# Loading the q and k weights into both partition halves, pairs of x blocks, and a new order, in an attention plus gMLP kernel

## The chip, the cores and the metric

The kernel runs on one core of one Trainium2 chip. The metric is the device time of one execution in microseconds (us), lower is better. Each run has a profiled span (first to last instruction), in most runs some 1.8 us shorter than its time, and the mean clock that TensorE was granted (1.0 is full speed). A run more than 1.5% above the fastest of the same kernel is called slow and left out of the ratios. "PE" is TensorE. The kernel before takes 255.0 us, the median of three runs (254.49 to 255.3).

## The reference, cut to what matters

```python
def reference(A_x, A_wqkv, A_wo, B_x, B_w_in, B_w_sp, B_b_sp, B_w_out):
    # S = 2048 tokens, D = 448, 16 heads of 28; bf16
    x = A_x
    h  = x + A(layernorm(x))     # q, k, v = x @ wqkv; each token attends to 8 keys,
                                 # itself and every second one before it; then @ wo
    h2 = h + B(layernorm(h))     # z = gelu(h @ w_in); g = w_sp @ layernorm(z[..., 896:]) + b_sp
    return h2                    # (z[..., :896] * g) @ w_out
```

The second part (gMLP with the 2048 x 2048 spatial weights) is dense matmul work and some 60% of the time. The change touches the start and the attention.

## The kernel before: the parts that matter

The program puts the two halves of the sequence (1024 tokens each) side by side: partitions 0 to 63 of the transposed, normalised x (`xh`) hold 64 features of the first half, partitions 64 to 127 the same features of the second. So each projection is two matmuls with 64 rows, and the weights must lie in both partition halves. Before, they were loaded once, with rows 0 to 383 across 128 partitions, and the PE copied each piece to both halves with a selector matrix (`dup`); ScalarE then moved it out of PSUM and padded each head from 28 to 32 columns.

```python
def ld_x(b, prio, eng="sp"):                       # one 128-token block of x
    t_x[b] = dma(eng, "x%d" % b, lambda e: e.dma_start(x_tm[:, b, :], X[128 * b:128 * b + 128, :]), ...)
# ... cut ...
t_w["qk", 0] = dma("act", "wqk0", lambda e: e.dma_start(
    stqk[:, 0:3, :], A_wqkv[0:384, 0:2 * D].rearrange("(c p) n -> p c n", p=128)), ...)
t_w["qk", 1] = dma("sp", "wqk1", lambda e: e.dma_start(stqk[0:64, 3, :], A_wqkv[384:448, 0:2 * D]), ...)
# ... cut ...
for h in hs:                                       # copies one piece to both halves
    iss("pe", lambda e, h=h: e.matmul(psum[:, bk[h] * 512:bk[h] * 512 + D], dup[64 * h:64 * h + 64, :],
                                      stqk[64 * h:64 * h + 64, j, c0:c0 + D]), ...)
# ... cut: ScalarE (one piece: VectorE) copies PSUM to wqp or wkp, 28 of every 32 columns ...
NWARM = 11                                         # idle matmuls at the very start
# ... cut ...
pace = [by[n % i] for i in range(4, NT) for n in ("exp%d_0", "mask%d", "ot%d")]
chain([t_wsp[b][0] for b in S_ORDER], pace, depth=2)   # spatial weights' transposing loads
```

x is normalised block by block on VectorE (`bn1`, `nrm1`). Blocks 0 to 2 of each half are transposed by the PE (`tT1`), blocks 3 to 7 by transposing DMA loads on SyncE's queue (`tD1`). One fixed list per engine gives the order of everything (`dp..` are the weight copies on the PE, `rp..` their padding, `mmq`, `mmk` and `mmv` the projections, `mml` logits, `ev..` evictions from PSUM):

```python
ORDER = {
    "sp":  """xhalo x0 x3 x11 x10 x1 x2 wqk1 x9 ... tD1_3 x4 x5 tD1_6 tD1_7 tD1_5 tD1_4 wsp0_0 ...""",
    "dve": """... bn1_14 mask0 bn1_15 bn1_5 bn1_4 nrm1_6 nrm1_14 nrm1_7 nrm1_5 nrm1_15 nrm1_13 evk1_1 nrm1_4 nrm1_12 ...""",
    "act": """x8 wqk0 rsh rs1_0 wv1 rpk1 rpk0 rpk2 ev1_0 rpk3 rpq0 rpq1 rpq2 evk0_0 ...""",
    "pe":  """warm dpk1 dpk0 tTh dpq0 dpk2 tT1_0 ... mmk0_0 dpq2 mmk0_2 mmq0_0 mmq0_2 tT1_2 tT1_1 mml0_00 mml0_01 mmv0 ...""",
}   # cut
```

The softmax here doesn't subtract the row's maximum and nothing guards it: scores larger than these inputs give would overflow.

## Time and profile before

| | kernel before |
|---|---|
| time, median of 3 | 255.0 us |
| profiled span, granted clock | 254.4 us, 1.000 |
| q and k weights landed | 6.75 us (the large part) |
| first q or k projection | 11.07 us |
| dense part, PE full | from 97.76 us to the end |

A profile line of a stretch gives its start and end, its length, then the busy time (and count) of PE, PE weight loads, VectorE, ScalarE and GpSimd, then the granted clock, the mean share of the 16 DMA engines that were busy, and GB/s. The chain is the work that ended last, followed backwards: each line is a start, a length, and what it was. The text below shows these views of the kernel before. One more of them is needed later, the same stretches microsecond by microsecond while the q and k weights fly (6 to 7) and after them (8 to 9):

```profile
6.00:7.00 1.00, 0.20 (x2) 0.11 (x4) 0.74 (x2) 0.00 (x0) 0.00 (x0) 1.00 1.09 371
...
8.00:9.00 1.00, 0.80 (x9) 0.49 (x9) 0.93 (x4) 1.00 (x3) 0.44 (x2) 1.00 1.07 258
```

The DMA engines are as busy in one as in the other; what differs is how much a busy engine moves.

### The profile page before, as it was taken

What the parts mean: (1) busy time and instruction counts of PE and PEld (TensorE: products, weight loads), DVE (VectorE), ACT (ScalarE), POOL (GpSimd) and SP (SyncE); (2) the same over time, 40 slices, a digit from 0 to 9 for tenths busy, and PEclk for the clock granted to TensorE, in tenths of its full rate; (3) what the DMA queues carried; (4) which work ended last, traced back from release to release, by engine and by line L of the source; (5) the groups of instructions that cost most, each with busy time, mean ns of one, the idle gap of its engine ahead of it and who ended that gap; (6) DMA issues with size and microseconds to landing.
All of it is one profiled execution on the core that took longest, in us unless ns stands there. A gap on an engine that the chain in (4) does not pass through costs nothing.

```text
span 254.4 us, 6475 instructions
## 1 busy us (share of the span) xinstructions
PE 240.2 (94%) x2906; PEld 120.0 (47%) x2917; DVE 144.4 (57%) x281; ACT 89.4 (35%) x105; POOL 27.7 (11%) x72
## 2 busy tenths in 40 slices
PE   7699979899997999999999999999999999999995
PEld 2375544455754544444444444444444444444452
DVE  7997755668796869998694013064700214424743
ACT  3878445555866785875644000000000000000000
POOL 5404300001020102201531000000000000000000
PEclk9999999999999999999999999999999999999999
DMA  6980892135688784399999900006000000010122
GB/s 218 260 107 4 156 153 67 21 78 143 118 116 84 125 129 73 72 130 194 231 186 170 201 3 0 3 0 124 0 3 18 0 0 0 25 50 0 54 66 82
DMA packets 55412, 22.03 MB, mean 87 GB/s; under 512 B 46664, under 2 KB 55256, under 8 KB 55384
## 3 DMA queue, kind: packets, MB, share of 16 engines
q1 hardware_dynamic: 51952, 16.79, 37.0%
q10 hardware_dynamic: 3432, 4.82, 9.0%
q8 instruction: 23, 0.38, 0.7%
q14 instruction: 5, 0.04, 0.1%
HBM read 8.39 MB, written 1.84 MB: 40 GB/s over the span
## 4 chain that ended last, share of the span: by engine, by line
PE 86%; DMA 5%; ACT 4%; DVE 3%; issue 1%; ACTq 0%
PE psum L1105 38%; PE psum L807 9%; PE psum L1134 8%; PE psum L1068 8%; PE psum L1005 8%; PE psum L985 4%; PE psum L847 3%; PE psum L882 3%; DMA xh<-tring 3%; DMA z2p<-in_A_wqkv_dram 2%; ACT reg L650 2%; PE psum L931 2%; ACT reg L895 1%; DVE reg L902 1%; PE psum L911 1%; DVE reg L949 1%
## 5 line engine op out<-in xcount | busy, mean ns | idle before, releaser
L1115 DVE TENSOR_TENSOR ub<-psum,reg 128x512 bf16<-128x512 f32 x28 | 18.7, 688 | 59.3 <-PE psum L1105 59.0
L1105 PE MATMUL psum<-reg,z2p 128*128 128x512 bf16 x218 | 48.8, 379 | 0.3
L1105 PE MATMUL psum<-wspT_lo,z2p 128*128 128x512 bf16 x219 | 48.1, 379 | 0.4 <-issue 0.2
L1105 PEld LDWEIGHTS psum<-wspT_lo,z2p 128*128 128x128 bf16 x224 | 21.8, 98 | 26.6 <-DVE z2p L1052 0.4
L1105 PEld LDWEIGHTS psum<-reg,z2p 128*128 128x128 bf16 x224 | 21.9, 98 | 26.1
L807 PE MATMUL psum<-xh,reg 64*128 64x128 bf16 (+3 forms) x336 | 26.9, 306 | 2.9 <-DMA xh<-tring 1.9
L650 ACT ACTIVATE reg<-psum 128x896 bf16<-128x896 f32 (+5 forms) x26 | 20.7, 851 | 7.2 <-PE psum L807 5.2
L1005 PE MATMUL psum<-w_in,xh 64*128 64x448 bf16 x224 | 22.7, 349 | 0.4 <-DVE reg L949 0.4
L895 ACT ACTIVATE reg<-psum 128x928 bf16<-128x928 f32 x18 | 17.0, 944 | 15.9 <-PE psum L847 7.1
L1134 PE MATMUL psum<-reg 128*128 128x448 bf16 x112 | 22.3, 352 | 0.1
L1068 PE MATMUL psum<-xh,w_in 64*128 64x512 bf16 x196 | 21.8, 376 | 0.0
L1142 DVE TENSOR_TENSOR tring<-psum,x_tm 128x448 bf16<-128x448 f32 x16 | 9.9, 622 | 17.9 <-PE psum L1134 17.8
L1036 DVE BATCH_NORM_STATS2 st<-z2p 128x6 f32<-128x448 bf16 x32 | 17.7, 609 | 3.9 <-ACT z2p L1030 3.9
L669 DVE BATCH_NORM_STATS2 st<-x_tm 128x6 f32<-128x448 bf16 x32 | 19.4, 606 | 0.4 <-DMA x_tm<-in_A_x_dram 0.3
L807 PEld LDWEIGHTS psum<-xh,reg 64*128 64x128 bf16 x336 | 13.2, 94 | 12.4 <-DMA xh<-tring 2.0
L656 POOL TENSOR_TENSOR rs<-rs,nhalf 128x2 f32<-128x2 f32 x23 | 16.6, 722 | 2.0
L1078 ACT ACTIVATE reg<-psum 128x1024 bf16<-128x1024 f32 x14 | 13.9, 1024 | 7.4 <-PE psum L1068 7.4
L652 DVE CAST reg<-psum 128x1024 bf16<-128x1024 f32 (+3 forms) x11 | 12.0, 1095 | 7.8 <-PE psum L807 6.2
L655 POOL TENSOR_SCALAR rs<-mv 128x2 f32<-128x2 f32 x23 | 5.2, 227 | 102.6 <-DVE mv L670 83.7
L1134 PEld LDWEIGHTS psum<-reg 128*128 128x128 bf16 x112 | 11.0, 98 | 10.6
L902 DVE TENSOR_TENSOR reg<-reg,mband 128x1856 bf16<-128x1856 bf16 x9 | 10.1, 1124 | 9.6 <-ACT reg L895 9.6
L1005 PEld LDWEIGHTS psum<-w_in,xh 64*128 64x128 bf16 x224 | 10.6, 94 | 10.3 <-issue 0.6
(68 smaller groups left out, 212.6 us busy)
## 6 DMA issues: line engine op xcount, KB each, us to landing
w_in<-in_B_w_in_dram ACTq DMA_DIRECT2D x4, 448.0 KB, 6.0
out_dram<-tring SPq DMA_DIRECT2D x16, 112.0 KB, 1.7
x_tm<-in_A_x_dram SPq DMA_DIRECT2D x15, 112.0 KB, 5.0
w_in<-in_B_w_in_dram ACTq DMA_DIRECT2D x4, 336.0 KB, 4.1
reg<-in_B_w_out_dram SPq DMA_DIRECT2D x1, 784.0 KB, 5.9
z2p<-in_A_wqkv_dram ACTq DMA_DIRECT2D x1, 672.0 KB, 5.5
reg<-in_B_b_sp_dram SPq DMA_DIRECT2D x1, 512.0 KB, 5.7
reg<-in_A_wqkv_dram ACTq DMA_DIRECT2D x1, 392.0 KB, 7.3
```

What stands on the lines that cost most here:

```text
L650: iss("act", lambda e: e.activation(dst, src, AF.Copy), reads=rd, writes=wr, after=after)
L656: iss("pool", lambda e: e.tensor_tensor(dst, dst, nh, ALU.pow), reads=rr + [r_nhalf], writes=rr)
L669: iss("dve", lambda e: e.bn_stats(st[:, b, :], x_tm[:, b, :]), reads=[r_x[b]], writes=[rl[b]])
L807: iss("pe", lambda e, c=c, s=s, gi=gi, lhs=lhs: e.matmul(psum[:, bk[s] * 512 + cw * gi:bk[s] * 512 + cw * gi + cw], lhs, xh[64 * s:64 * s ...
L895: iss("act", lambda e: e.activation(E[:, es[0], 2 * n:2 * n + 2, :], pair_view(lb, 0, 8 * JW), AF.Exp, scale=SCALE), reads=[r_bank[lb[0]], ...
L1005: iss("pe", lambda e, c=c, s=s: e.matmul(psum[:, zb[s] * 512:zb[s] * 512 + D], xh[64 * s:64 * s + 64, c, XO + 128 * u:XO + 128 * u + 128], ...
L1036: iss("dve", lambda e, b=b: e.bn_stats(st3[:, b, k, :], z2p[:, b, D * k:D * k + D]), reads=[r_z2[b][k]], writes=[r_st3[b][k]])
L1068: iss("pe", lambda e, c=c, s=s: e.matmul(psum[:, bk[s] * 512:bk[s] * 512 + 512], w_in[64 * s:64 * s + 64, c, 128 * f:128 * f + 128], xh[64 ...
L1078: iss("act", lambda e: e.activation(z1p[f].rearrange("p (s t) -> p s t", s=2)[:, :, 512 * ch:512 * ch + 512], pair_view(bk, 0, 512), AF.Ge ...
L1105: iss("pe", lambda e, b=b: e.matmul(psum[:, gb[0] * 512:gb[0] * 512 + 512], z2p[:, b, 128 * f:128 * f + 128], src[:, b, 512 * (tc % 2):512 ...
L1115: iss("dve", lambda e: e.tensor_tensor(ub[:, us_[0], :], psum[:, gb[0] * 512:gb[0] * 512 + 512], bb[:, 512 * tc:512 * tc + 512], ALU.add), ...
L1134: iss("pe", lambda e, f=f: e.matmul(psum[:, wb[0] * 512:wb[0] * 512 + D], z1p[f][:, 128 * m:128 * m + 128], w_out[:, f, :], start=(f == 0) ...
```

## The change

The intent: take the copying of weights off the PE and out of PSUM, by loading them twice, straight to both halves, and padding from SBUF on whichever of three engines is free; load x in larger pieces; hold the spatial weights' transposes back to tile 6 of the attention; and use the new order that the program's own planner makes of this. The diff, cut to its core:

```diff
-        def ld_x(b, prio, eng="sp"):
-            t_x[b] = dma(eng, "x%d" % b, lambda e: e.dma_start(x_tm[:, b, :], X[128 * b:128 * b + 128, :]), ...)
+        def ld_x(u, prio, eng="sp"):
+            t_x[u] = t_x[u + 8] = dma(eng, "x%d" % u, lambda e: e.dma_start(
+                x_tm[:, u:u + 9:8, :], X.rearrange("(s b p) d -> p b s d", s=2, p=128)[:, u]), ...)
 # ... cut ...
-        t_w["qk", 0] = dma("act", "wqk0", ...)      # rows 0 to 383, 128 partitions
-        t_w["qk", 1] = dma("sp", "wqk1", ...)       # rows 384 to 447
+        for j, (c0, c1) in enumerate(((0, 4), (4, NC7))):
+            for sd, eng in ((0, "sp"), (1, "act")):
+                t_w["qk", sd, j] = dma(eng, "wqk%d%d" % (sd, j), lambda e, sd=sd, c0=c0, c1=c1: e.dma_start(
+                    stqk[64 * sd:64 * sd + 64, c0:c1, :], A_wqkv[64 * c0:64 * c1, 0:2 * D].rearrange("(c p) n -> p c n", p=64)), ...)
 # ... cut: dup and its 14 matmuls removed ...
+                    copy(tk[0].eng, (wkp if p == "k" else wqp)[:, c0:c1, :].rearrange("p c (h d) -> p c h d", d=32)[:, :, :, 0:DH],
+                         stqk[:, c0:c1, o:o + D].rearrange("p c (h d) -> p c h d", d=DH), ...)   # on VectorE, ScalarE or GpSimd
 # ... cut ...
-        pace = [by[n % i] for i in range(4, NT) for n in ("exp%d_0", "mask%d", "ot%d")]
+        pace = [by[n % i] for i in range(6, NT) for n in ("exp%d_0", "mask%d", "ot%d")]
 # ... the order lists, cut to their heads ...
-    sp: xhalo x0 x3 x11 x10 x1 x2 wqk1 x9 ... tD1_3 x4 x5 tD1_6 tD1_7 tD1_5 tD1_4
+    sp: xhalo x1 x0 x3 wqk01 wqk00 x2 x7 wv0 x4 x5 x6 tD1_3 tD1_6 tD1_5 tD1_4 tD1_7
-    act: x8 wqk0 rsh rs1_0 wv1 rpk1 rpk0 rpk2 ev1_0 rpk3 rpq0 rpq1 rpq2 evk0_0
+    act: tab wqk11 rsh wqk10 wv1 rs1_0 rpk3 rpq2 rpq1 ev1_0 rpk0 rpk1 ev1_1 evq0_0
-    dve: ... bn1_14 mask0 bn1_15 bn1_5 bn1_4 nrm1_6 nrm1_14 ... nrm1_13 evk1_1 nrm1_4 nrm1_12
+    dve: ... bn1_12 nrm1_6 nrm1_14 mask0 nrm1_5 bn1_4 nrm1_13 nrm1_7 nrm1_4 nrm1_15 nrm1_12
-    pe: warm dpk1 dpk0 tTh ... mmk0_0 dpq2 mmk0_2 mmq0_0 mmq0_2 tT1_2 tT1_1 mml0_00
+    pe: warm tTh tT1_0 tT1_1 mmq0_0 mmq0_2 mmk0_2 mmk0_0 tT1_2 mmv0 mml0_00
```

## The prediction

> **What bounds the kernel now.** I read the page first, for the busy shares and the slices.
>
> ```profile
> PE 240.2 (94%) x2906; PEld 120.0 (47%) x2917; DVE 144.4 (57%) x281; ACT 89.4 (35%) x105; POOL 27.7 (11%) x72
> PE   7699979899997999999999999999999999999995
> PEclk9999999999999999999999999999999999999999
> GB/s 218 260 107 4 156 153 67 21 78 143 118 116 84 125 129 73 72 130 194 231 186 170 201 3 0 3 0 124 0 3 18 0 0 0 25 50 0 54 66 82
> ```
>
> TensorE is busy for 94% of 254.4 us at the full clock. Its low digits lie in the first two slices (up to 12.7 us), in the sixth and near 80 us. Only holes of this kind can be closed by moving loads and repacking. So I cut the span into four stretches (view of busy time by stretch: us, then PE, PEld, DVE, ACT, POOL, clock, DMA share, GB/s; the first of these rows is from another answer).
>
> ```profile
> 0.00:11.07 11.07, 7.30 (x37) 2.65 (x39) 9.12 (x27) 6.12 (x11) 5.42 (x28) 1.00 0.87 233
> ...
> 29.80:37.20 7.40, 5.54 (x176) 3.45 (x168) 5.35 (x5) 3.46 (x4) 0.00 (x0) 1.00 1.16 170
> 37.20:97.76 60.56, 56.32 (x1380) 30.66 (x1382) 43.57 (x61) 40.27 (x44) 4.56 (x10) 1.00 0.61 101
> 97.76:133.70 35.94, 35.82 (x350) 16.96 (x352) 30.98 (x76) 22.30 (x26) 10.06 (x22) 1.00 0.82 146
> 133.70:251.60 117.90, 117.30 (x549) 54.59 (x558) 39.76 (x77) 2.80 (x3) 0.70 (x1) 1.00 0.20 41
> ```
>
> From 97.76 us (the last output projection of attention, then gMLP) the PE is full to the end: 153.8 us that no load shortens. The attention stretch has 60.56 - 56.32 = 4.2 us idle, and 29.8 to 37.2 has 1.9. Then the chain that ended last, for the start:
>
> ```profile
> 1.25 5.50 DMA z2p<-in_A_wqkv_dram
> ...
> 6.80 0.41 PE psum L764 x2
> 7.23 2.54 ACT reg L650 x3
> 9.77 0.81 ACT xh L650
> 10.58 2.07 ACT reg L650 x3
> ...
> 12.69 2.52 PE psum L807 x84
> ...
> 29.80 7.36 DMA xh<-tring
> ```
>
> The start is a chain: the q/k weights land at 6.75, the PE copies them to both halves (L764), ScalarE pads seven of the eight pieces out of PSUM, and projections (L807) begin at 11.07, in earnest at 12.69. Later the chain runs through the transposing loads of normalised x. Last, the PE's waits within 11 to 98 us:
>
> ```profile
> PE psum L911 <- DVE reg L902: 2.2, 3, 1.1
> PE psum L807 <- DMA xh<-tring: 1.9, 1, 1.9
> PE psum L807 <- ACT reg L650: 1.1, 2, 0.6
> ```
>
> One DMA wait of 1.9 us, 1.1 us of waits for ScalarE copies (repacking among them), and 2.2 us of waits for the masked exponentials, which the change doesn't address.
>
> **What the Trainium skill says.** "DMA: Bandwidth & Descriptors", section "Rules for kernel authors", advises against two transfers to disjoint partition halves, since both spread over the same 16 DMA engines and serialize. So the second copy of the weights is paid in full, in bytes; the trace agrees in so far as the early DMA share is 1.0 to 1.1, with nothing idle to take it. "SBUF — State Buffer", section "SBUF: two separate sides", says that VectorE in a 2-port mode and GpSimd lock one shared port pair against each other for a whole instruction. The changed kernel puts three GpSimd copies beside VectorE's normalising; no copy of this kind is in the trace before, so it doesn't show it. "GPSIMD Engine Reference", section 3.1, puts simple one-input work at 1.03 cycles an element; the trace has a GpSimd memset of 1792 elements in 1.59 us, 0.89 ns each, which agrees. An 896-element copy is then an estimated 0.9 to 1.2 us.
>
> **The change, part by part.**
>
> (1) Removed: 14 matmuls on L764 and the three building steps of their selector on GpSimd (0.20 + 1.16 us). The matmuls take 0.55 + 4 x 0.36 + 0.54 = 2.5 us of PE, but all except one pair (0.36 us, at 11.88) lie before 11.07, where the PE waits for data anyway. Direct gain: about 0.4 us.
>
> (2) Added: a second copy of the q/k weights, 0.80 MB more on a start that carried 3.4 MB. The measured rates are 376 GB/s from 4 to 7 us, when the 1792-byte weight rows fly, and 234 GB/s from 7 to 11, with 896-byte rows. By 4.0 us the queues had moved 0.02 + 0.19 + 0.28 = 0.49 MB, a ramp that I keep. Before the last weight piece lands, SyncE's queue must move 14 kB + 3 x 229 + 344 + 459 = 1.50 MB and ScalarE's 0.80, plus perhaps a third of its v weights (0.13): 2.44 MB. The remaining 1.95 MB at some 350 GB/s need 5.6 us: the weights are complete at about 9.8 us, not at 6.75 to 9.
>
> (3) Repacking from SBUF, by the instruction order of the changed kernel: four of eight pieces need only the first loaded part (about 7.6 us) and are done by the time the rest lands. After 9.8 ScalarE does one q piece (0.85), the eviction of block 0 (0.92) and two k pieces (0.85 each); GpSimd does one q piece. So q projections start at 9.8 + 1.77 + 0.1 = 11.7, k at 13.4; the 112 of them take 0.96 + 2.52 = 3.5 us as before, to 15.2. Then a transpose (0.5) and the first v projection (1.45), which now stands before the logits and fills the PE while ScalarE evicts (0.92 + 4 x 0.60 from 13.3, so 16.6). The first half of the logits (0.44) ends at 17.1 + 0.44 = 17.5. Before, the same set of work ended at 18.33: **0.8 us gained**.
>
> (4) x in pairs, and order: the transposing load of block 3 now stands behind all x loads. In total 4.25 MB; 1.8 MB after 9.8 at 234 to 260 GB/s end at about 17, and its own landing follows at 18 to 19 us, where the PE wants it at 17.5. If pairs run faster than single blocks there is no wait; else it eats up to 1.5 us. I take **-0.5 us**, net +0.3 for the start.
>
> (5) Blocks 6, 5, 4, 7: block 6 is now normalised ahead of the first mask. Four transposes took 24.94 to 37.16 before, beside 0.46 MB of MLP weights issued at 29.97 that now come after the exponentials of tile 2. Issued from an estimated 20.8 us, the last at 25.5, at an estimated 2.2 us each, they land by 31. The PE's work up to the projections that need them is 37.2 - 1.9 - 0.3 = 35.0 us. The wait of 1.87 us goes: **+1.9 us**.
>
> (6) Spatial-weight transposes from tile 6 instead of 4: the one SyncE queue is free for the second-norm transposes until about 75 us; 16 loads of 262 kB at 150 GB/s take an estimated 28 us, over by some 110 us, and are wanted at about 130. Hidden. The gain is a cleaner queue only, as no wait of the PE on that queue after 37.2 shows.
>
> (7) The order of attention is new throughout, and one more gMLP unit (six, not five) fills it. Work per tile in its second half is nearly even: PE about 6.3 us; ScalarE 1.9 + 2.0 + 0.9 + 0.9 = 5.7; VectorE 1.1 + 1.2 + 1.1 + 1.6 + 0.9 = 5.9. With three engines so close, idle PE time doesn't vanish; of 4.2 us I expect 0.6 back (between -1 and +2).
>
> Sum: 0.3 + 1.9 + 0.6 = 2.8 us off 255.0: **252.2 us**.
>
> **The rivals.**
>
> A: the doubled weights make the start later. If both queues keep to 250 GB/s, 1.95 MB take 7.8 us; everything in (3) slides by 2.2 us, the start loses 1.4 and the block-3 transpose stays a wait. For it: the DMA share is already over 1.0, and rows of 896 bytes lie between. Against it: 376 GB/s measured with just these 1792-byte rows. Time: 253.5 to 255.
>
> B: the removed DMA wait comes back as a wait for ScalarE or VectorE. With the transposes early, the PE meets the evictions of q and k instead; logits of tiles 4 and 5 now stand right after the last q projections, whose eviction lies late on ScalarE. A wait of 1 to 1.7 us there would take most of (5). Time: 253.5 to 254.
>
> C: the new order, made for a truer picture of the loads, closes most of the holes in attention: 2.5 to 3.5 of 4.2 us, with the start at +1. For it: three waits for one mask (2.2 us) are matters of order. Time: 248.5 to 250.
>
> D: GpSimd's copies and VectorE's normalising lock each other out. At most three copies of about 1 us, early, where VectorE is 90% busy: up to 1 us later.
>
> **Range and chances.** The full stretch of 153.8 us bounds the change from both sides; only some 14 us of PE idle time and the start can move. A and B together give 255 to 256, C gives 248.5 to 250, so I take 249.2 to 255.2 for 8 in 10. Faster by over 2% needs under 249.9, so nearly all of C: 0.22. Slower by over 2% (over 260.1) needs a new wait of 5 us: 0.05. Within 2%: 0.73.
>
> **What would show it.** Step 2: the last q/k weights landing at 9.3 to 10.3 us. Step 3: q projections from about 11.7, and the first logits about 17, after the first v projection. Step 4: a PE wait on the transposed x of 0 to 1.5 us at 17 to 19. Step 5: no such wait between 28 and 40, and the first 512-column projection at 34 to 35.5 us instead of 37.2. Step 6: none on it after 60. Step 7: 3 to 5 us idle in attention, the last output projection ending at about 96.5 with six gMLP units done, then 152 to 153 us of full PE. It would be wrong if the first projections came after 13.5, if the dense part showed holes (norms on VectorE, 86% busy there, falling behind), or if attention lost over 2 us to evictions.

## The result, and the profile after

The changed kernel takes **258.37 us**, the median of four runs (257.36 to 259.01); the kernel before took 255.15 in the same rounds (254.49 to 256.08). The ratio is 1.012, with a 95% interval from 1.0074 to 1.0166: 1.2% slower. A ratio is the mean time of one kernel's fast runs over the mean of the other's fast runs of the same rounds, so it is not quite the ratio of the medians. That lies within the 2% that count as the same time, and outside the predicted range. The outputs are correct. A second series on another chip gave 257.41 us and 1.0023 (below).

First the page of the changed kernel: the busy shares, and the slices of the PE, of its clock and of the bytes.

```profile
PE 243.2 (95%) x2903; PEld 124.8 (49%) x2903; DVE 138.9 (54%) x275; ACT 93.0 (36%) x108; POOL 29.3 (11%) x71
PE   6279999999999999999999999999999999999995
PEclk9759999999999999999999999999999999999999
GB/s 176 251 262 21 76 104 63 48 56 76 95 100 149 110 103 69 165 136 224 172 215 187 173 162 41 41 3 0 0 0 3 0 0 0 3 18 72 54 66 82
```

The holes in the sixth slice and near 80 us are gone: from the fourth slice on the PE is full. But the second slice has fallen from 6 tenths to 2, and the clock row, all 9 before, reads 7 and 5 in slices two and three. Busy time is up by 3 us although the weight copies (2.5 us) are gone: at half the clock the same matmuls are busy for longer, as the 112 first projections below show. The stretches that the prediction used:

```profile
0.00:11.07 11.07, 4.48 (x12) 1.51 (x13) 7.38 (x23) 3.59 (x7) 5.40 (x24) 0.91 0.84 201
...
29.80:37.20 7.40, 7.40 (x206) 4.98 (x204) 4.12 (x6) 4.64 (x6) 0.00 (x0) 1.00 0.69 122
37.20:97.76 60.56, 59.02 (x1462) 33.83 (x1456) 42.13 (x59) 40.80 (x47) 5.55 (x12) 1.00 0.44 88
```

The attention is idle for 60.56 - 59.02 = 1.5 us where it was 4.2, and the stretch from 29.8 to 37.2 for nothing where it was 1.9. All the loss lies ahead of 29.8. The chain for the start says what it waited for, and the PE's work in order of time what that did:

```profile
3.66 9.14 DMA z2p<-in_A_wqkv_dram
...
12.82 0.95 ACT reg L645
13.77 0.82 ACT xh L645
...
14.72 5.47 PE psum L792 x112
```

```profile
1.75 4.46 PE L639 MATMUL psum<-warm 128*128 128x512 bf16 x11 [1.75 <-DVE warm L604]
11.05 0.35 PE L728 MATMUL psum<-ident,thalo 16*128 16x16 bf16 x7 [4.84 <-DVE thalo L720]
```

The last copy of the q and k weights is issued at 3.66 us and lands at 12.80. The projections start at 14.72, not at 11.7, and take 5.47 us, not 3.5 (0.96 + 2.52 before). The PE's 11 idle matmuls end at 6.21, and then it has nothing for 4.84 us. The first v projection ends at 22.07; the prediction had 17.1, and before it and half of the logits had ended at 18.33.

The same two facts microsecond by microsecond (last three numbers: clock, DMA share, GB/s):

```profile
8.00:9.00 1.00, 0.00 (x0) 0.00 (x0) 0.96 (x4) 0.22 (x1) 0.52 (x2) 1.00 1.07 229
9.00:10.00 1.00, 0.00 (x0) 0.00 (x0) 0.94 (x3) 0.97 (x4) 0.94 (x2) 0.53 1.07 201
```

At 9 us the clock drops to a half, and it stays at 0.50 until past 19 (0.85 from 19 to 20). And while weight rows of 1792 bytes are in flight, with all DMA engines busy, the queues move 201 to 229 GB/s, not the 371 of before. (From 5 to 6 us, with pairs of x in flight beside the weights, they reach 376.)

From the PE's waits the transposing DMA has gone, and so have the VectorE waits of the masks. In the attention only two small waits are left, both for the VectorE step that scales the attention output (L934):

```profile
PE psum L792 <- ACT xh L645: 1.4, 1, 1.4
...
PE psum L970 <- DVE reg L934: 0.5, 1, 0.5
PE psum L896 <- DVE reg L934: 0.3, 1, 0.3
```

**Two theories.** T1: the start is late for two separate reasons, weights that land some 3 us late because a load into 64 partitions moves at about 200 GB/s, and a PE left idle long enough for its clock to halve until 19.5 us. Together they cost more than the better attention gives back. T2: the second copy is only more bytes; x and v loads compete with it, or pairs of x blocks bring the first block late, and the clock is a symptom without cost of its own. A part of both is what the attention gained and why.

### The profile page after: what moved, and what is told of

Read it like the earlier page. It is cut to its first block, busy times and chain, and to the rows that moved or that the text cites.

```text
span 255.6 us, 6458 instructions
## 1 busy us (share of the span) xinstructions
PE 243.2 (95%) x2903; PEld 124.8 (49%) x2903; DVE 138.9 (54%) x275; ACT 93.0 (36%) x108; POOL 29.3 (11%) x71
## 4 chain that ended last, share of the span: by engine, by line
PE 91%; DMA 4%; ACT 1%; DVE 1%; SPq 1%; issue 1%
PE psum L1090 38%; PE psum L792 11%; PE psum L990 8%; PE psum L1053 8%; PE psum L1119 8%; PE psum L970 5%; PE psum L832 5%; PE psum L867 4%; DMA z2p<-in_A_wqkv_dram 4%; PE psum L916 3%; PE psum L896 1%; DVE reg L934 1%; ACT reg L645 1%; SPq L563 1%; ACT reg L880 0%
## 5 line engine op out<-in xcount | busy, mean ns | idle before, releaser
L792 PE MATMUL psum<-xh,reg 64*128 64x128 bf16 (+3 forms) x336 | 28.9, 330 | 1.4 <-ACT xh L645 1.4
L1053 PE MATMUL psum<-xh,w_in 64*128 64x512 bf16 x196 | 22.5, 376 | 0.0
L664 DVE BATCH_NORM_STATS2 st<-x_tm 128x6 f32<-128x448 bf16 x32 | 19.5, 610 | 5.1 <-DMA x_tm<-in_A_x_dram 5.0
L792 PEld LDWEIGHTS psum<-xh,reg 64*128 64x128 bf16 x336 | 15.5, 108 | 10.1 <-POOL reg L647 1.6
L645 ACT ACTIVATE reg<-psum 128x896 bf16<-128x896 f32 (+4 forms) x22 | 18.3, 853 | 5.8 <-PE psum L792 2.5
L1119 PEld LDWEIGHTS psum<-reg 128*128 128x128 bf16 x112 | 11.0, 98 | 10.5
L680 DVE TENSOR_SCALAR tring<-x_tm,mv,rs 128x448 bf16<-128x448 bf16 x32 | 14.8, 490 | 0.5 <-POOL rs L651 0.5
```

The costliest lines, as they stand in the source:

```text
L645: iss("act", lambda e: e.activation(dst, src, AF.Copy), reads=rd, writes=wr, after=after)
L664: iss("dve", lambda e: e.bn_stats(st[:, b, :], x_tm[:, b, :]), reads=[r_x[b]], writes=[rl[b]])
L680: iss(tn[n].eng, lambda e: e.tensor_scalar(tring[:, h[0], :].rearrange("p (c s f) -> p s c f", c=NC7, s=2)[:, n], x_tm[:, b, :].rearrange( ...
L792: iss("pe", lambda e, c=c, s=s, gi=gi, lhs=lhs: e.matmul(psum[:, bk[s] * 512 + cw * gi:bk[s] * 512 + cw * gi + cw], lhs, xh[64 * s:64 * s ...
L1053: iss("pe", lambda e, c=c, s=s: e.matmul(psum[:, bk[s] * 512:bk[s] * 512 + 512], w_in[64 * s:64 * s + 64, c, 128 * f:128 * f + 128], xh[64 ...
L1119: iss("pe", lambda e, f=f: e.matmul(psum[:, wb[0] * 512:wb[0] * 512 + D], z1p[f][:, 128 * m:128 * m + 128], w_out[:, f, :], start=(f == 0) ...
```

## The experiments

Sixteen kernels ran. Since the granted clock differs from run to run in every kernel, the mean clock stands beside each span where a comparison needs it. A mean clock of 0.993 over 255 us is 2 x 0.007 x 255 = 3.6 us at half clock.

### The changed kernel again

The same text, on another chip beside its own runs of the kernel before.

> The changed kernel unaltered, for a comparison on one chip with the three runs beside it. It should read a clock of 0.978 to 0.980, with the first v projection ending at about 22 us, and 1.010 to 1.014 of the kernel before. If it comes out within 0.5% of the kernel with more warm-up matmuls (0.996 in the first batch), the halved clock is not worth 2 us.

257.41 us, ratio 1.0023 (0.9949 to 1.0097), below the expected 1.010 to 1.014; spans 256.6, 254.7, 255.3 and 255.8, all with a clock of 0.978 or 0.980. The runs of before had spans of 253.4 to 258.0, with clocks from 1.0 down to 0.986. So the changed kernel has a mean clock of 0.978 to 0.980, as of one such half-clock stretch, in all its eight runs (mean span 255.8), while the kernel before has one in some runs: with clock 1.0 its spans average 253.9 (17 of them over all rounds), at 0.992 to 0.993 255.3 (11). The size of the loss thus depends on the state of the runs of before: 1.2% in the first series, 0.2% in this. In full-clock runs of before against any of the changed kernel it is 1.9 us.

### Idle matmuls in the gaps of the start

```diff
-NWARM = 11
+NWARM = 33                      # idle 512-column matmuls at the start
-    pe: warm tTh tT1_0 tT1_1 mmq0_0
+    pe: warm tTh tT1_0 tT1_1 warm2 mmq0_0      # warm2: six more of them
```

> The changed kernel with 33 instead of 11 warm-up matmuls and 6 more after the first transposes, so that TensorE never idles for long before the first projections. Theory 1 (the clock): the idle stretch from 6.2 to 11.05 us halves the granted clock from 9.5 to 19.5 us, and the 112 first projections take 5.5 us instead of 3.5. Then the clock reads 1.00 here, these projections take about 3.5 us, the first v projection ends at about 20.1 us instead of 22.1, and the time falls by about 2 us against the changed kernel, to 1.003 to 1.006 of the kernel before. Theory 2 (only the late landing of the weights counts): the clock may rise but the time moves by less than 0.5 us.

255.72 us, ratio 0.9957 (0.9901 to 1.0013); spans 255.1 (clock 0.993), 253.7, 253.5 and 254.2 (0.999 or more). The PE's order of work in the start of the profiled run:

```profile
5.56 5.87 PE L639 MATMUL psum<-warm 128*128 128x512 bf16 x24
...
15.02 3.35 PE L800 MATMUL psum<-xh,reg 64*128 64x128 bf16 x112 [0.65 <-ACT xh L653]
...
18.80 1.52 PE L840 MATMUL psum<-reg,xh 64*64 64x448 bf16 x28
```

The 112 projections take 3.35 us again instead of 5.47; the first v projection ends at 20.25 instead of 22.07, though the weights land a little later (13.04). At full clock the mean span is 253.8, against 255.8 of the changed kernel (256.1 and 255.6 in its two series, on other chips): **the half clock costs 2.0 us**, and work that computes nothing gets it back; within the profiled runs the first v projection ends 1.8 us earlier. The ratio is better than the 1.003 to 1.006 expected, as the runs of before were slower in these rounds. That part of T1 is shown.

### The same bytes into 128 partitions

Wrong (relative error 0.948): the four weight loads keep their rows and queues and, in sum, their bytes (the smaller two have 256 and 128 rows, not 192 each), but land across 128 partitions.

```diff
-  stqk[64 * sd:64 * sd + 64, c0:c1, :], A_wqkv[64 * c0:64 * c1, 0:2 * D].rearrange("(c p) n -> p c n", p=64)
+  stqk[:, WC[sd, c0][0]:WC[sd, c0][1], :], A_wqkv[0:128 * (...), 0:2 * D].rearrange("(c p) n -> p c n", p=128)
```

> The changed kernel with the same bytes, rows of 1792 bytes and order of weight loads, but each load written to all 128 partitions instead of 64 (the weights are then wrong on purpose, and so is the result). If a load into 64 partitions is what moves slowly, the last weights land at about 10 us instead of 12.8, at 330 GB/s or more, the projections begin about 2.5 us earlier, and the time falls by 2.5 to 4 us. If only the number of bytes ahead counts, they land at 12.3 to 13 us again and the time stays within 0.5 us of the changed kernel.

256.94 us, ratio 1.0003 (0.9953 to 1.0054). The same microseconds as above:

```profile
8.00:9.00 1.00, 0.00 (x0) 0.00 (x0) 0.94 (x3) 0.97 (x4) 0.87 (x2) 0.50 1.05 393
9.00:10.00 1.00, 0.00 (x0) 0.00 (x0) 0.99 (x4) 0.61 (x1) 0.84 (x2) 0.50 1.07 393
```

393 GB/s where the changed kernel had 229 and 201, at the same share of busy engines. But the last weights land at 12.44 us only (12.80 before): 3.24 MB had moved by then instead of 2.73, since x and v loads behind them on the same queues took the freed rate. The rate half of T1 is shown; what it is worth is not, and T2's competition is not out either. The next two runs settle that.

### Later loads held back

The warmed kernel, with the v weights of ScalarE's queue and the pairs of x from the fourth on held until SyncE's second weight copy has landed.

```diff
-    act: tab wqk11 rsh wqk10 wv1 rs1_0 rpk3 rpq2 rpq1 ev1_0 rpk0 rpk1 ev1_1
+    act: tab wqk11 rsh wqk10 rs1_0 rpk3 rpq2 rpq1 ev1_0 rpk0 rpk1 wv1 ev1_1
+    ld_x(2): reads=[r_stqk[0][0]]
```

> The changed kernel with the longer warm-up, and with the v weights of ScalarE's queue and the x pairs from the fourth on held back until the second copy of the q/k weights has landed. If the weights came late because later transfers shared the DMA engines with them (2.7 MB had moved when the last weights landed at 12.8 us, 2.3 MB being needed), they land at 10.5 to 11.5 us here and the first projections begin at about 13 us instead of 15.0. If the rate of these rows alone is the limit, they land no earlier than 12.3. The time may not follow: the v weights and the transposed block 3 then land later, and the PE may wait for those.

258.65 us, ratio 1.0083 (1.0001 to 1.0165). The last weights still land at 12.9 us, with only some 2.35 MB moved. Near the end of the weights the queues run dry:

```profile
9.00:10.00 1.00, 1.00 (x6) 0.48 (x5) 0.97 (x3) 0.97 (x4) 0.94 (x2) 1.00 1.07 199
...
12.00:13.00 1.00, 0.61 (x10) 0.50 (x9) 0.44 (x2) 0.08 (x1) 0.05 (x1) 1.00 0.31 45
```

With almost nothing else to carry, the rate stays at 199 to 213 from 7 to 10 us (276 in the next). So competition is not what makes the weights late, and T2 falls for them. Holding loads back only made v and x late afterwards.

### Held back, and into 128 partitions

Both edits together (wrong, as above).

> This is the run with later loads held back, with the four weight loads landing in 128 partitions instead of 64 (same bytes, same rows of 1792 bytes, wrong result on purpose). Theory A (a load into one half of the partitions moves at about 200 GB/s whatever else runs): with 128 partitions the 2.3 MB that stand ahead of the second weight copy move at 320 to 390 GB/s, the last weights land at 9.5 to 10.5 us instead of 12.9, the q projections start at about 12 instead of 15, and the profiled span is 1.5 to 3 us under that of the held run (256.7), so about 254. Rival (the rows of 1792 bytes, or the issue on two queues, are what is slow): last weights still after 12 us, span within 1 us of 256.7.

The last weights land at 10.28 us, by the chain:

```profile
3.30 6.98 DMA z2p<-in_A_wqkv_dram
```

That is in the range expected of the first theory (9.5 to 10.5) and close to the 9.8 of the prediction: with 128 partitions the rate comes near the prediction's (341 to 385 GB/s from 6 to 9 us), with 64 it does not. **The 64-partition destination makes the weights 2.6 us late** (12.9 against 10.28). The time, 257.36 us (ratio 0.9973, 0.9862 to 1.0084), says less: the profiled span of 256.9 missed the 254 expected, at a clock of 0.987 and with x late behind the hold; the two full-clock runs had 254.3 and 254.0. The projections begin at 13.51 us, 1.3 us before the held run's 14.82 and not at the expected 12: ScalarE's eviction of block 0 is done at 12.39, but the six idle matmuls stand ahead of the projections and end at 13.58. So the landing is shown by this run, and its worth is not; 14.82 - 12.39 = 2.4 us at the first projections is an estimate from these two traces.

### x ahead of the weights

The warmed kernel, with ScalarE's first weight load issued after the statistics of the halo.

```diff
-    act: tab wqk11 rsh wqk10 wv1
+    act: tab rsh wqk11 wqk10 wv1
```

> The changed kernel with the longer warm-up, and with ScalarE's first weight load issued only after the halo's statistics, so that three pairs of x have the DMA engines to themselves at first. If the first x pair landed at 5.7 us because it shared them, it lands by 4.3 us here and the first transpose on the PE can begin at about 9.5 us instead of 11. The weights then land 0.3 to 1 us later than 13.1, and the first projections, which wait for them, begin at 15.0 to 16 us: no gain, 0 to 1 us lost. If x were the bound of the first projections, they would begin 1 us or more earlier.

258.89 us, ratio 1.0093 (1.0002 to 1.0185). ScalarE's first step on block 0 came 1.8 us earlier (7.04 against 8.87 us), but the last weights landed at 15.3 and the projections began at 17.26. What the first projections wait for in the changed kernel is the weights; x is not.

### Only the pairs of x, in the kernel before

```diff
-    sp: xhalo x0 x3 x11 x10 x1 x2 wqk1 x9 x14 x6 ...
+    sp: xhalo x0 x3 x1 x2 wqk1 x6 ...           # each load a pair of blocks; act: x8 dropped
```

> The kernel before with x loaded as pairs of blocks on SyncE's queue and nothing else changed. If pairs hold up the first block, the first statistics of x begin at 4 us or later instead of 3.4, the block-0 transposes come 0.7 to 1.5 us later than 8.5, but the first projections, which the weights bound, stay at about 11 us: the time is within 0.5 us of the kernel before. If pairs move faster than single blocks, the last of x lands earlier than 16.6 us. If pairing is the cause of the late start, the first projections begin after 12.5 us and the time rises by 1.5 us or more.

262.23 us median; two of four runs slow. The fast ones, both at a clock of 0.987, give a ratio of 1.0139 (1.004 to 1.0238), which is called unclear. In the profiled run, a slow one, the first pair lands at 5.69 us, where the first single block of before was there at 3.4; the first projections start at 12.27 us instead of 11.07, at half clock (from 9.4 us, with the weight copies in place); and a transposed block is waited for by 2.65 us near 41. In that start, where weights are early, x is what is waited for, and pairs cost.

### Only the pairs undone, in the changed kernel

```diff
-    sp: xhalo x1 x0 x3 wqk01 wqk00 x2 ...
+    sp: xhalo x1 x9 x0 x8 x3 x11 wqk01 wqk00 x2 x10 ...     # single blocks again
```

> The changed kernel with each pair of blocks of x loaded as two single blocks again, in the same order on the same queue; nothing else differs. Theory A (the first pair has twice the bytes, so that its first block is there later, and the wait for it is the PE's idle stretch that halves the clock): first block lands at about 4.2 instead of 5.7 us, the first transpose comes at 9.5 to 10 instead of 11.05, but the weights still land near 12.8; time 0.3 to 1.5 us under the changed kernel's 257.9 if the clock stays at half, and about 255.7 if it comes back. Rival (pairs cost nothing at the start, since statistics and the weights are what is waited for): first transpose within 0.3 us of 11.05, time within 0.5 us. Sixteen issues instead of eight on the queue may delay the weight loads behind them by up to 1 us, which would hide a gain.

258.76 us, ratio 1.0057 (0.9976 to 1.0138), spans 256.4 to 258.4 at 0.973 to 0.979. VectorE's first statistics of x begin at 5.83 us (5.71 with pairs), the first transpose is at 11.15 us (11.05 with pairs), and the weights, behind more issues, land at 14.44. So the pairs are not what makes x late in the changed kernel: the rival named in this run is right, and T2's second half falls too. In the run with x ahead of the weights these statistics begin at 3.98 us, so it was ScalarE's first weight load that x had waited behind. The time says nothing of the pairs, as the weights came 1.6 us later. The two pair runs together suggest that the same part can cost in one start (1.4% above, clock included) and not in another, by what that start waits for.

### The start of before with the order of after

If the loss is all in the start, the two can be parted: the kernel before (its loads, its weight copy on the PE) up to the first transposes, then the changed kernel's attention order and tile 6.

```diff
 # kernel before, with the order lists cut and joined:
+    pe:  (before, up to tT1_1)  then (after, from mmv0)
+    act: (before, up to ev1_1)  then (after, from evv0)
+    dve, sp, pool: likewise from nrm1_6, tD1_6, rs1_6;   pace: range(6, NT)
```

> The start of the kernel before (weights loaded once and copied by TensorE, single blocks of x, its order up to the first logits), then the order of the changed kernel from the first v projection on, and its pace of spatial transposes. If the changed kernel loses 4.2 us at the start and gains about 3 us after it, this one ends the first v projection at about 18 us, has no wait on the transposed x near 30 to 37 us, and takes about 3 us less than the kernel before: a ratio of 0.987 to 0.990. Rival: the new order only looks good because its late start gives VectorE and the transposing loads more time; then waits come back, and the ratio is 0.996 to 1.002.

253.47 us, ratio 0.9862 (0.9806 to 0.9919), correct: faster than both kernels. Spans 252.1, 249.9, 251.5 and 251.9; only the second at full clock. The first v projection ends at 18.15 us and no DMA wait is left. The profiled run had half-clock stretches at 10.7 to 14 and 68 to 72 us.

### The same with three idle matmuls in the start

```diff
+    three idle 512-column matmuls ahead of the first k projection
```

> The start of the kernel before with the changed order of attention (as in the third run of the first batch), and three idle matmuls of 512 columns put into the wait of TensorE before the first k projection. If too little work from 7 to 10.8 us is what halves the clock from 10.7 to 14 us in some runs, the clock reads 1.00 there; the first v projection ends 0.5 to 1 us earlier than 18.15 us, and the ratio is 0.980 to 0.986. Rival: the extra matmuls delay the k projections by as much; then 0.986 to 0.990.

**252.57 us** (251.93 to 253.06), ratio 0.9828 (0.9757 to 0.9899), correct; spans 251.0, 251.2, 250.2 and 250.6. In the profiled run the clock is 1.00 throughout the start, and the first v projection ends at 17.20 us:

```profile
10.21 0.82 PE L803 MATMUL psum<-warm 128*128 128x512 bf16 x3 [0.62 <-ACT reg L651]
10.96 0.96 PE L811 MATMUL psum<-xh,reg 64*128 64x128 bf16 x28
```

This is 1.7% under the kernel before and about 2% under the changed one; whether it is faster than before by 2% stays unclear. That the three idle matmuls keep the clock is not shown: of the five profiled runs that have them, two (the void one and the one with late transposes, below) have half clock from 10 or 11 us to 13 or 14 us, as the one profiled run of this order without them had. Four of the runs that follow build on it.

### Spatial transposes let go from tile 4 again

```diff
-        pace = [by[n % i] for i in range(6, NT) ...
+        pace = [by[n % i] for i in range(4, NT) ...
```

> The fastest run so far (start of the kernel before, attention order of the changed one, three idle matmuls) with the spatial transposes let go from tile 4 again instead of tile 6. If the move to tile 6 is worth nothing by itself (the prediction's part six), the time stays within 0.5 us of 252.6. If the order of the attention gained because these transposes no longer stand ahead of the second-norm transposes on the DMA queue, it rises by 1 to 2 us and a wait for a DMA of 1 us or more shows on the PE between 40 and 100 us.

252.62 us, ratio 0.9819 (0.9732 to 0.9906); full-clock spans 250.3 and 250.1. No DMA wait shows between 20 and 100 us. Within 0.1 us of the version with tile 6 (252.57, in other rounds): the tile is worth nothing by itself here.

### The transposes alone, in the kernel before

```diff
-    sp:  tD1_3 x4 x5 tD1_6 tD1_7 tD1_5 tD1_4
+    sp:  tD1_3 x4 x5 tD1_6 tD1_5 tD1_4 tD1_7
-    dve: mask0 bn1_15 bn1_5 bn1_4 nrm1_6 nrm1_14 nrm1_7 nrm1_5 nrm1_15 nrm1_13 evk1_1 nrm1_4 nrm1_12
+    dve: bn1_15 bn1_5 nrm1_6 nrm1_14 mask0 nrm1_5 bn1_4 nrm1_13 evk1_1 nrm1_7 nrm1_4 nrm1_15 nrm1_12
```

> The kernel before with one part of the change alone: normalisations and transposes of blocks 6, 5, 4, 7 in that order, ahead of the first mask and of the statistics of block 4, with the PE's order as before. If the prediction's term is right (the 1.87 us wait for a DMA near 37 us goes and is kept to the end), the wait goes or falls under 0.3 us and the time falls by 1.5 to 2 us, to a span of 252.3 to 252.7 at full clock. Rival (the gain needs the PE's new order; the wait is only moved, or the later mask makes a new one of its own on the PE near 17 to 22 us): under 0.7 us of gain.

A miss: 256.42 us, ratio 1.0014 (0.995 to 1.0078). The wait did not go, it grew from 1.87 to 2.94 us. VectorE's work in order of time, then the PE's:

```profile
27.75 0.98 DVE L652 CAST reg<-psum 128x796 bf16<-128x796 f32 x1 [3.03 <-PE psum L807]
28.65 1.74 DVE L685 TENSOR_SCALAR tring<-x_tm,mv,rs 128x448 bf16<-128x448 bf16 x4
```

```profile
38.13 1.69 PE L807 MATMUL psum<-xh,reg 64*128 64x512 bf16 x14 [2.94 <-DMA xh<-tring]
```

The eviction `evk1_1`, left on VectorE ahead of the last four normalisations, waits 3.03 us for the PE, and the transposes wait behind it. In the changed kernel that eviction is on ScalarE. The diff shows it only as a name missing from one list and added to another.

### The transposes alone, with that eviction behind them

```diff
-    dve: ... nrm1_13 evk1_1 nrm1_7 nrm1_4 nrm1_15 nrm1_12
+    dve: ... nrm1_13 nrm1_7 nrm1_4 nrm1_15 nrm1_12 evk1_1
```

> As the run with the transposes alone in the kernel before, but with the VectorE's eviction of one k projection (which there stood ahead of the last four normalisations and waited 3.03 us for the PE) put behind them. If the late transposes came from that eviction, the four normalisations end near 27.3 instead of 30.4 us, the last transpose lands some 3 us earlier, the 2.94 us wait before the first 512-column projection goes (under 0.3 us), and the time falls 1.5 to 2 us under the kernel before (span 252.3 to 252.7 at full clock). If the PE's order is what gains, the wait goes but the time comes back later and the span stays above 253.5 at full clock.

254.13 us median of six, ratio 0.9922 (0.9853 to 0.9991). The profiled run (span 256.0), its order of events:

```profile
27.24 1.33 DVE L685 TENSOR_SCALAR tring<-x_tm,mv,rs 128x448 bf16<-128x448 bf16 x3 [0.76 <-POOL rs L656]
29.20 0.99 DVE L652 CAST reg<-psum 128x796 bf16<-128x796 f32 x1 [0.63 <-PE psum L807]
```

The normalisations end at 28.6, against 30.4 in the run above, although this run was 1.4 us behind that one at the first mask, and the wait before the first 512-column projection is 0.42 us. The four full-clock runs have 252.2, 252.2, 252.3 and 252.5, in or 0.1 us under the expected range; the four of before in the same rounds 253.1 to 254.0, mean 253.5. So **the early transposes are worth 1.2 us alone**, under the 1.5 to 2 expected, given that nothing stands ahead of the normalisations.

### The new attention order, with the transposes late

The fastest version with the SyncE, VectorE and GpSimd orders of those blocks put back as before.

> The fastest version (start of before, attention order of the changed kernel, three idle matmuls) with the normalisations and transposes of blocks 6, 7, 5, 4 put back to the order of the kernel before. If the transposes are worth 1.9 us, this is 1.9 us slower than the fastest version (span about 252.2 at full clock against 250.3) with a DMA wait of 1.5 to 2 us before the first 512-column projection. If the PE's new order is what gains, the span stays within 0.7 us of 250.3.

254.13 us, ratio 0.9929 (0.9871 to 0.9987); spans 251.5, 252.6 and 252.2 at 0.993, mean 252.1, and 253.3 at 0.987. The runs of the fastest version and its two near copies at 0.993 average 251.5. So with the PE's new order late transposes cost some 0.7 us only, and a wait of 0.52 us is all that shows: neither 1.9 us nor nothing. The profiled run had half clock in its start and was 1.8 us behind the fastest version at the first v projection, which can have shortened that wait, and the span at full clock was not measured: the 0.7 rests on three runs. With 0.7 or with the 1.2 above, the order of the attention is the larger term.

### Idle matmuls in the attention, twice

Half-clock stretches also occur in the attention, in some profiled runs of several kernels. In a profiled run of the fastest version the clock is 0.50 from 67 to 70 us, although the PE is busy all along; ahead of it lie 3.1 us of small matmuls on parts of the array (columns of the last row: clock, DMA share, GB/s):

```profile
63.62 1.49 PE L935 MATMUL psum<-reg 64*32 64x58 bf16 x64
65.05 1.71 PE L886 MATMUL psum<-reg 32*64 32x58 bf16 x48
```

```profile
68.00:69.00 1.00, 1.00 (x16) 0.55 (x12) 0.75 (x3) 1.00 (x3) 0.13 (x1) 0.50 0.00 0
```

The first try, two idle matmuls between these two groups:

> The fastest run so far with two idle 512-column matmuls put into the run of small tiled matmuls of tile 6 (about 65 us). Theory (about 3.5 us of small matmuls with 58 columns on quarter tiles drop the granted clock to half for some 3.5 us in part of the runs): the clock stays 1.00 there in all four profiled spans, mean clock 0.999 or more, and the spans lie at 250.2 to 250.8, each about 0.8 to 1.0 us under a run of the fastest version that has the dip (251.0, 251.2). Rival (the dips have another cause): at least two of four spans still show a mean clock of 0.993 or less, and the idle matmuls cost 0.4 us.

It is void: a loop variable was read after the loop had ended, and the trace has no idle matmul there. It serves as a repeat of the fastest version on another chip: 253.58 us, ratio 0.9821 (0.9719 to 0.9924), clocks 0.986, 1.0, 0.993, 0.993. The second try, with the variable bound:

```diff
-                    def em(a=a, lb=lbs[n], rkq=rkq, n=n, half=half):
+                    def em(i=i, a=a, lb=lbs[n], rkq=rkq, n=n, half=half):
+                        for _ in range(2 if (i, n, half) == (6, 0, 0) else 0):
+                            iss("pe", ...)          # idle matmul, 512 columns
```

> The fastest version with two idle 512-column matmuls (0.43 us) truly put into the run of small tiled matmuls of tile 6 near 65 us. Theory (a run of about 3 us of matmuls with 58 columns on parts of the array halves the granted clock for some 3.5 us): no half clock between 60 and 75 us in the profiled run, and at least five of six spans at a mean clock of 0.993 or more with most at 0.999 or more. In the runs of the fastest version without it, seven of eight clocks were 0.993, 0.993, 1.0, 0.999 and, in its unintended repeat, 0.986, 1.0, 0.993, 0.993. Rival (other cause): half the runs or more at 0.993 or less, with the drop in the same place.

252.34 us (251.89 to 253.12, six runs), ratio 0.9862 (0.9819 to 0.9905). The profiled run has no half clock from 60 to 73 us. Clocks 1.0, 0.993, 1.0, 1.0, 0.999 and 1.0: five of six at full clock, against five of twelve in the three series without the idle matmuls. This fits the theory and doesn't prove it, also because a mean clock does not say whether the start or the attention was slow, and one profiled run without them (tile 4 again) kept the full clock too. The time hardly tells the versions apart: mean span 250.7, against 250.8 for the first series of the fastest version and 251.1 for all three. The cause of these stretches stays open.

## Why the prediction was wrong

**What it put together.** In spans at full clock, the kernel before has 253.9 us, the kernel with the old start and the new attention order 250.4 (ten runs of the fastest version and its near copies), the warmed changed kernel 253.8, and the changed kernel, always with its half-clock stretch, 255.8. So the new order in the middle gains 3.5 us, the new start at full clock loses 3.4, the half clock loses 2.0: 253.9 - 3.5 + 3.4 + 2.0 = 255.8. The sum closes by construction, as each term is the difference of two neighbours. The series ran on several chips, on which the full-clock spans of before average 253.5 to 254.4, so each term is good to about half a us. The prediction had 2.5, then a gain of 0.3, and no third term.

**Step 1**, the removed copying, held as far as it goes: no such matmul lay on the path afterwards.

**Step 2 failed.** It took "some 350 GB/s" from the microseconds in which the old 1792-byte rows fly, and read the row length as the reason. But the old load spanned 128 partitions and the new ones span 64; into 64, 199 to 229 GB/s were measured, into 128 again 375 to 393. The last weights landed at 12.80 us, not 9.8. (Two slips beside it: the step's own sum, 4.0 + 5.6, gives 9.6; and 0.36 MB had moved by 4.0 us, not the 0.49 that it kept from before.) Rival A had the effect (250 GB/s, everything 2.2 us later), but with rows and shares as the reason, not the partitions. The prediction cited a page's rule on disjoint halves and drew from it only that bytes are paid twice. The Trainium skill, "SBUF — State Buffer", section "Door 1: The DMA port swizzle", says what was missed: 64 partitions reach half of the ports, 196 GB/s against 328 for 128 partitions at 1 MiB. The runs agree on the first figure and lie above the second.

**Step 3 failed by that and by the clock.** It took 3.5 us for the 112 projections "as before". They took 5.47 at half clock. The removed weight copies had been most of what the PE did between 6 and 11 us (7.30 busy us up to 11.07 before, 4.48 after), and the first transposes, 7.29 us before, came at 11.05. That the gap is the cause is shown by the run that filled it; that the copies alone would have prevented it is not, as the kernel before with pairs has the copies and lost the clock too. The Trainium skill, "TensorE: Matmul & The Clock Gate", section "What's actually happening", gives half the clock after an idle window of about 3.4 us and full clock only after as long a busy one; here the clock fell 2.9 us into 4.84 idle us (2.3 to 3.4 us in four profiled runs of this start, the ends of matmuls being modelled), no later than that and mostly sooner, and half clock lasted until 19 to 20 us, some 5 us into the projections. Step 1 called the copies free because they lay beside a wait. They were not free to remove with nothing in their place.

**Step 4** expected a wait on block 3's transpose. None came; the start was later than those loads.

**Step 5** named a gain of 1.9 us. The wait went, as it said. By itself the early transposes are worth 1.2 us, and with the new order 0.7. It also missed that one eviction had to leave VectorE first.

**Step 6 held**: tile 4 or tile 6 makes no difference (250.3 and 250.1 against 250.2 and 250.6 at full clock).

**Step 7 was mis-sized**: 0.6 us (-1 to 2) expected, about 2.8 measured, as 3.5 for all less the 0.7 of the transposes (2.3 if one takes off the 1.2). Idle time in the attention fell from 4.2 to 1.5 us. Rival C (2.5 to 3.5 of 4.2) was right here. The argument against, that three nearly even engines cannot be packed tighter, did not hold. Rival B's waits for evictions did not show, and rival D's clash of GpSimd and VectorE did not either: GpSimd's two 896-element copies took 0.93 us each, as estimated, and the 448-element one 0.56.

**The dense part** was full in both, as said. It began later by what the start had lost: the first 512-column projection came at 38.61 us, not at 34 to 35.5, and the last output projection ended near 100.2, not 96.5.

What stays open: how the 3.4 us of the start at full clock divide between the weights' 2.6 us of lateness (2.4 at the first projections by the estimate above) and the rest (an order that leaves the PE waiting for ScalarE), and what halves the clock in the attention.

## What to carry to other kernels

When a load changes the partitions that it lands in, take its rate from a trace of a load of that width, not from one with the same row length. Before removing PE work that lies beside a wait, ask what the PE does in its place: a gap of some 5 us in the start cost 2 us of clock afterwards, and idle matmuls bought it back. And where a change has a good and a bad half, run them apart: the new order with the old start was faster than either kernel.

## What the Trainium skill lacked or had wrong

- "TensorE: Matmul & The Clock Gate" ties a clock that falls in mid-kernel to waits of the PE and to short idles between groups of matmuls. Here it fell to 0.50 for some 3.5 us with the PE busy for all of each microsecond by the profile, behind 3.1 us of 58-column matmuls on parts of the array. The page has nothing on such matmuls; with two idle matmuls among them five of six runs kept the full clock throughout, without five of twelve. Nor does it say how little work counts as idle: in the old start with the new order the clock fell at 10.8 us, in the second of two microseconds with the PE busy for 0.46 and 0.38.
- The same page puts the ramp at under 1% of a typical span. The 2.0 us of 255.8 here are 0.8%, which agrees; between two tuned kernels this was as large as the whole difference (1.9 us at full clock of before). Removing work from beside a wait can open such a stretch.
- "SBUF — State Buffer" has 328 GB/s for one 128-partition transfer of 1 MiB; with several in flight, 367 to 393 GB/s were seen here. Its figure for 64 partitions, 196, agrees with the 199 to 229 here.
- No page that was read gives a rate for x in pairs of blocks against single blocks. Beside the old weight load, single blocks left the queues at 258 GB/s from 8 to 9 us and pairs at 369 (in a slow run). It didn't help, as the first block then came at 5.69 us and not at 3.4.
